# The opening of an attention-and-MLP kernel: three query groups on the incoming keys, one tile's statistics on ScalarE, value projections held back

## The chip, the cores and the metric

The kernel runs on one core of one Trainium2 chip. A core has five engines that run side by side: TensorE (PE, matrix products), VectorE (DVE, elementwise work and reductions), ScalarE (ACT, functions such as the exponential), GpSimd (POOL) and SyncE (SP, which here issues every DMA transfer). The metric is the device time of one execution in microseconds (us); less is better. Times are given for several executions of the same kernel, and one further execution was recorded by the hardware profiler.

## The reference: what is computed

One batch of S = 2048 tokens with D = 1024 features goes through a block of two branches. All inputs are bf16.

```python
xn  = layernorm(x)                        # over the 1024 features, no scale or shift
# branch A: attention with 32 heads of 32
q, k, v = split(xn @ wqkv)                # wqkv is 1024 x 3072
p   = softmax(q @ k.T * 32 ** -0.5)       # per head, 2048 x 2048, not masked
s   = (p @ v, heads side by side) @ wo
# branch B: an MLP on a second normalisation
y   = layernorm(xn)
g   = silu(gelu_tanh(y @ w1 + b1) @ w2 + b2)   # 1024 -> 3584 -> 1024
out = x + s * g
```

The exponentials of the softmax are 32 x 2048 x 2048 elements. They run on ScalarE in 1024 instructions of 128 partitions by 1024 elements.

## The kernel before

The program is not written as loops that run on the chip. A planner in Python (`_Plan`) is given operations with the data that they read and write, an assumed duration and a priority. `run` plays them through with these assumed times and fixes one order for each engine; `settle` derives the semaphore waits, and `emit` writes the instructions. On the chip each engine works through its list strictly in that order: an instruction whose data has not come yet holds up all that stand behind it on its engine.

**Tiles.** Tokens are cut into 16 tiles of 128 (`t`), or 8 pairs of 256 (`n`, `kp` for keys, `qb` for queries). Heads are cut into 8 groups of four (`hg`). A *unit* is one head group, one query pair and one key pair: eight score matmuls (line 809) into two pairs of PSUM banks, then two exponentials (line 818) into a slot of `P`. A *product* (`pvs`, kind "pv") collects over the eight key pairs of one query pair: eight small matmuls a unit with V (`v_fn`) and the sums of the softmax. The sums come either from eight more small matmuls a unit with ones (`plain`, line 893), or from pairwise adds on VectorE (`tree`, lines 835 and 852) and a few matmuls at the end. Only one product is open at a time.

**The opening.** For each tile `load_x` (line 614) brings 128 rows. VectorE takes statistics in two halves (line 759, `bn_stats`) and joins them (line 761); the epsilon is added (line 765), GpSimd raises to the power -1/2 (line 767), and VectorE normalises into a buffer in `gw` (line 736). The tile is then turned so that features lie on partitions (`xnT`): tiles 0 to 3 by TensorE (line 723) with a copy on ScalarE (line 726), the other tiles by a DMA transpose that SP issues (line 740). From `xnT` come, for the first head group, the keys of a token pair (`k_item`, copied out of PSUM by ScalarE on line 712), the queries (`q_item`, copied by VectorE on line 702, or 512 tokens at once with `qk_item`, line 692), and the values of the first two head groups (`v_item`, copied by VectorE on line 680). Projections of 128 rows run through `mm` (line 608). These items, the products and later the MLP's items share PSUM banks 6 and 7; the scores have banks 0 to 5.

In the first head group two query pairs are worked on together while the keys come in. The order of the units is

```python
order0 = [(0, 0), (0, 1), (1, 0), (1, 1)] + [(qb, kp) for kp in range(2, NKP) for qb in range(2)]
```

as (query pair, key pair), so 16 units, and each has its own slot of `P`: ten are the slots of the whole run, three lie in the buffer of `w1` and three in that of `w2`, which are not needed yet. From the 17th unit on, slots 0 to 9 are used in turn. The other six query pairs and the other seven head groups follow one after the other, with their sums in trees on VectorE.

**What sets the order.** For TensorE the planner prefers a score unit that is ready, then a product or an item by position (`pos`) and due time; an item of kind "pro" with `pos` below 0.2 (keys and queries) goes ahead of a product. While TensorE has nothing ready, it is given *fillers*, small matmuls on the identity (line 658). For VectorE, ScalarE and SP it takes the ready operation with the lowest priority number and, among equals, the one that was added first. When it chooses, an operation whose input has only just been produced counts as ready some 115 to 220 ns after the producer's end, and another one may be started in the meantime. The loads of tiles 10 to 15 wait for earlier tiles to be normalised.

The planner also has pseudo-random jitter, by 30 us of planned time and by the index of the operation; it is switched on for the third such stretch only.

## Time and profile before

| | us |
|---|---|
| median of three runs | 1039.95 |
| lowest, highest | 1039.22, 1040.24 |
| the profiled execution's own time | 1039.56 |
| span of the profiled execution | 1037.7 |
| ScalarE busy | 1014.2 |
| TensorE busy | 999.4 |
| VectorE busy | 948.0 |
| mean granted TensorE clock | 0.998 of full speed |

How to read the profile: PE is matmul, PEld the load of matmul weights (it overlaps PE), SPq the issue of DMAs by SyncE. A row of the timeline gives the start in us, the duration of the merged instructions in us, engine, line, operation, written and read tile, and the count `x`; a bracket holds the idle time of that engine just before, and what ended it. Neighbouring instructions overlap a little, so a merged row is shorter than count times the mean of one. A row of busy time by stretch gives the stretch and its length, then the busy time and instructions of PE, PEld, DVE, ACT and POOL, the granted clock, the share of the DMA engines in use and GB/s. A row of a group of instructions gives count, busy us in all, mean ns of one, and the idle time before them with what ended it. A row of DMA issues gives count, size and the median us from issue to landing. The chain that ended last is followed back from the last instruction, at each step to what released it.

### The profile page before, as it was taken

To read this page: it belongs to the slowest core of one execution; us is meant where nothing else is said; L and a number is where in the kernel's file an instruction comes from. 1 tells how busy PE (TensorE), PEld (TensorE's weight loads), DVE (VectorE), ACT (ScalarE), POOL (GpSimd) and SP (SyncE) were. 2 spreads that over 40 slices of the span, in tenths; PEclk is the share of its full clock that TensorE was granted. 3 is DMA by queue.
4 is the path that set the end of the run, shared out by engine and by line. 5 is a ranking of instruction groups with operands and counts; after the bars stand their busy time and mean duration, and the time that the engine had idled before them with its cause. 6 is when DMAs were issued, how large, how long until landed. Compare 5 with 4: busy or idle time off the path is not lost.

```text
span 1037.7 us, 31413 instructions
## 1 busy us (share of the span) xinstructions
PE 999.4 (96%) x14064; PEld 637.6 (61%) x14129; DVE 948.0 (91%) x1314; ACT 1014.2 (98%) x1089; POOL 11.0 (1%) x20
## 2 busy tenths in 40 slices
PE   9999999999999999999999999999999999999996
PEld 7556556666665676666565665666656655654442
DVE  8579999899899999987999999998999799788887
ACT  5899999999999999999999999999999999999996
POOL 1200000000000000000000000000000000000000
PEclk9999999999999999999999999999999999999999
DMA  8985747455656686456375677554456643573321
GB/s 191 206 224 169 190 131 209 122 150 160 180 164 167 174 227 175 129 159 176 106 174 153 179 203 183 164 161 139 135 156 190 197 139 141 165 235 117 111 75 52
DMA packets 318199, 167.99 MB, mean 162 GB/s; under 512 B 56688, under 2 KB 306032, under 8 KB 318064
## 3 DMA queue, kind: packets, MB, share of 16 engines
q1 hardware_dynamic: 318064, 165.98, 58.1%
q8 instruction: 111, 1.82, 0.8%
q14 instruction: 24, 0.20, 0.1%
HBM read 146.55 MB, written 12.06 MB: 153 GB/s over the span
## 4 chain that ended last, share of the span: by engine, by line
ACT 94%; DVE 3%; PE 2%; DMA 1%; issue 0%; POOL 0%; SPq 0%
ACT P L818 86%; ACT ut L1003 5%; ACT gw L1030 1%; DVE stats L759 1%; PE ps L608 1%; DMA hT<-in_A_x_dram 1%; ACT w1r L818 1%; ACT w2r L818 1%; DMA xnT<-gw 0%; DVE gw L736 0%; PE ps L809 0%; PE ps L603 0%; DVE hT L1247 0%; POOL lnp L767 0%; DVE mv L761 0%
## 5 line engine op out<-in xcount | busy, mean ns | idle before, releaser
L818 ACT ACTIVATE P<-ps 128x1024 bf16<-128x1024 f32 x1012 | 944.4, 1249 | 3.7 <-PE ps L809 3.7
L835 DVE TENSOR_TENSOR PA<-P 128x2048 bf16<-128x2048 bf16 x178 | 216.0, 1217 | 32.9 <-ACT P L818 31.9
L608 PE MATMUL ps<-yT,w1r 128*128 128x256 bf16 x1792 | 227.5, 273 | 0.2 <-DVE hT L988 0.2
L608 PE MATMUL ps<-w2r,hT 128*128 128x256 bf16 x1792 | 222.8, 273 | 1.8 <-DVE gw L1023 1.7
L809 PE MATMUL ps<-QKT 32*128 32x256 bf16 x4096 | 203.3, 273 | 16.4 <-ACT P L818 14.1
L852 DVE TENSOR_TENSOR PR<-PR,PA 128x2048 bf16<-128x2048 bf16 x178 | 215.5, 1212 | 1.3
L608 PEld LDWEIGHTS ps<-yT,w1r 128*128 128x128 bf16 x1792 | 163.9, 98 | 52.9 <-issue 28.7
L608 PEld LDWEIGHTS ps<-w2r,hT 128*128 128x128 bf16 x1792 | 163.4, 98 | 50.3 <-issue 30.2
L809 PEld LDWEIGHTS ps<-QKT 32*128 32x128 bf16 x4096 | 60.6, 92 | 148.9 <-ACT P L818 145.2
L603 PE MATMUL ps<-P,V 128*32 128x256 bf16 x4048 | 137.8, 274 | 0.6 <-ACT P L818 0.6
L608 PE MATMUL ps<-xnT,wqk 128*128 128x512 bf16 (+1 forms) x502 | 119.2, 364 | 4.3 <-issue 1.1
L603 PEld LDWEIGHTS ps<-P,V 128*32 128x32 bf16 x4048 | 96.2, 96 | 30.7 <-issue 21.4
L608 PE MATMUL ps<-wv,xnT 128*128 128x256 bf16 (+1 forms) x576 | 86.6, 285 | 2.2 <-DVE V L680 1.2
L608 PEld LDWEIGHTS ps<-xnT,wqk 128*128 128x128 bf16 x552 | 48.0, 98 | 53.0 <-issue 16.9
L988 DVE TENSOR_TENSOR hT<-ps,b1T 128x512 bf16<-128x512 f32 x112 | 76.6, 684 | 1.5 <-PE ps L608 0.8
L835 DVE TENSOR_TENSOR PR<-P 128x2048 bf16<-128x2048 bf16 x62 | 75.4, 1216 | 1.2 <-ACT P L818 0.2
L608 PEld LDWEIGHTS ps<-wv,xnT 128*128 128x128 bf16 x576 | 52.5, 98 | 24.6 <-issue 9.9
L1003 ACT ACTIVATE ut<-ut 128x2048 bf16<-128x2048 bf16 (+1 forms) x32 | 61.2, 1923 | 0.0
L692 DVE CAST QKT<-ps 128x512 bf16<-128x512 f32 x59 | 40.3, 683 | 3.0 <-PE ps L608 2.8
L907 DVE STREAM_TRANSPOSE nt<-ps 128x256 f32<-128x256 f32 x64 | 28.3, 443 | 11.8 <-PE ps L603 11.7
L1000 DVE TENSOR_TENSOR ut<-hT 128x2048 bf16<-128x2048 bf16 (+1 forms) x32 | 34.5, 1082 | 0.2
L1005 DVE TENSOR_TENSOR hT<-ut,hT 128x2048 bf16<-128x2048 bf16 (+1 forms) x32 | 34.5, 1079 | 0.1
(76 smaller groups left out, 535.5 us busy)
## 6 DMA issues: line engine op xcount, KB each, us to landing
w1r<-in_B_w_dram SPq DMA_DIRECT2D x112, 512.0 KB, 4.3
w2r<-in_B_w_dram SPq DMA_DIRECT2D x128, 448.0 KB, 4.3
hT<-in_A_x_dram SPq DMA_DIRECT2D x20, 256.0 KB, 3.7
wqk<-in_A_wqkv_dram SPq DMA_DIRECT2D x16, 256.0 KB, 3.4
yst<-in_A_x_dram SPq DMA_DIRECT2D x16, 256.0 KB, 4.6
g_scratch<-gw SPq DMA_DIRECT2D x32, 128.0 KB, 4.1
o_scratch<-ot SPq DMA_DIRECT2D x56, 64.0 KB, 3.6
xnT<-o_scratch SPq DMA_DIRECT2D x7, 512.0 KB, 5.9
```

What stands on the lines that cost most here:

```text
L603: ins = e.matmul(dst(j), lhsT=lhsT(j), rhs=rhs(j), start=start, stop=stop, tile_position=(0, 32 * j), skip_group_check=True)
L608: return e.matmul(dst, lhsT=lhsT, rhs=rhs, start=start, stop=stop, skip_group_check=True)
L692: dve(lambda e: e.tensor_copy(QKT[sl][:, which, tq * 512:(tq + 1) * 512], bank(it.bank)), c_ps(512), [], [(nm, sl, 2 * tq), (nm, sl, 2 * t ...
L809: ins = e.matmul(bank(b0[j], kk * 256, (kk + 1) * 256), lhsT=QKT[sl][32 * j:32 * j + 32, 1, kb * 128:(kb + 1) * 128], rhs=QKT[sl][32 * j:3 ...
L818: x = act(lambda e, h=h: e.activation(Pt[pi][:, 2 * h:2 * h + 2].rearrange("p j k q -> p (j k q)"), ps[:, pr[h] * 1024:(pr[h] + 1) * 1024] ...
L835: return dve(lambda e: e.tensor_tensor(dst[:].rearrange("p u j q -> p (u j) q"), src[:].rearrange("p u j k q -> p (u j) k q")[:, :, 0, :], ...
L852: return dve(lambda e: e.tensor_tensor(fl3(pr), fl3(pr), fl3(PA[i]), op=ALU.add), c_b16(2048), [("PA", i), tok], [tok], 3.2)
L907: dve(lambda e: e.transpose(nt_t[:], bank(pv.bank, 256, 512)), c_ps(256) + 120, [], [("nt",)], prio, pv)
L988: dve(lambda e: e.tensor_tensor(hT[:, hs], bank(it.bank).rearrange("p (k t) -> p k t", k=2), b1T[:, 2 * pi:2 * pi + 2].unsqueeze(2).to_bro ...
L1000: dve(lambda e: e.tensor_tensor(u_, x_, x_, op=ALU.mult), c_b16(n), hs_, [("ut", ui)], 3)
L1003: act(lambda e: e.activation(u_, u_, ACT.Tanh, scale=GC), c_acts(n), [("ut", ui)], [("ut", ui)], 1)
L1005: dve(lambda e: e.tensor_tensor(x_, u_, x_, op=ALU.mult), c_b16(n), [("ut", ui)] + hs_, hs_, 3)
```

## The change

The change touches the opening, and with it the order that the planner gives to everything behind.

1. *Loads.* Tiles 2 and 3 are loaded ahead of the key and query weights, where they came behind them.
2. *Statistics of tile 1.* They move from VectorE to ScalarE: a Copy and a Square over 1024 elements, each with an accumulated sum, give the mean and the mean square. Three operations of one column on VectorE form the variance. Tiles 2 and 3 now have a power of their own each, and the condition that held back tile 2's statistics until tile 1 is normalised is gone.
3. *ScalarE's copy of tile 1* out of PSUM is cut in two halves, and the data `xnT` is tracked by tile and by block of 128 features, so that projections can start on the first half.
4. *VectorE's order.* Aggregates get a better priority, and in the first 16 us of planned time the planner lets VectorE wait up to 130 ns (220 ns for a normalise) for a nearly ready operation of better priority rather than start a statistic. The assumed duration of a normalise goes from 60 to 118 ns over its base.
5. *Three query groups.* The third query pair joins from the third key pair on. Its first four units get four more slots of `P`, in memory not used yet (one in V, one in the second Q/K buffer, two in `hT` where tiles 6 to 9 were loaded), and its sums are done by `plain` on TensorE. The queries of pairs 2 and 3 become two items of 256 tokens in place of one of 512.
6. *Values.* Value item `n` of the first head groups is not offered until `6 + n` score units have been issued.

```diff
@@ pick
+            if e == "DVE" and best is not None and 1 <= best.prio <= 1.2 and t < 16000.0:
+                for r, _, o in soon[e]:
+                    if r < t + (220.0 if o.prio > 0.96 else 130.0) and o.prio < best.prio - 0.04 and not o.dead:
+                        wake(r, e)
+                        return None
@@ next_dense
-                if h < len(q):
+                if h < len(q) and q[h].hold <= S["s"]:
@@ the kernel
-        NTR, NWARM = 4, 8
+        NTR, NWARM, NG0, AT = 4, 8, 3, 1
...
+        Pt.append(V[:, 2].rearrange("p t n -> p (t n)").rearrange("p (j k q) -> p j k q", j=4, k=2))
+        Pt.append(QKT[1][:, 0].rearrange("p (j k q) -> p j k q", j=4, k=2))
...
+        for i in range(2):
+            Pt.append(h_flat[:, (3 + i) * 2048:(4 + i) * 2048].rearrange("p (j k q) -> p j k q", j=4, k=2))
...
-        load_x(0)
-        load_x(1)
+        for t in range(NTR):
+            load_x(t)
         wk0 = load_qk(0, 1)
         wq0 = load_qk(0, 0)
-        load_x(2)
-        load_x(3)
...
-            act(lambda e: e.activation(xnT[:, :, t * 128:(t + 1) * 128],
-                                       bankb(it.bank).rearrange("p (c t) -> p c t", c=DC), ACT.Copy),
-                c_act(1024), [tk], [("xnT", t)], 0, it)
+            for lo, hi in ((0, 4), (4, 8)) if t == 1 else ((0, 8),):
+                act(lambda e, lo=lo, hi=hi: e.activation(xnT[:, lo:hi, t * 128:(t + 1) * 128],
+                                                         bankb(it.bank)[:, lo * 128:hi * 128].rearrange("p (c t) -> p c t", t=128),
+                                                         ACT.Copy),
+                    c_act((hi - lo) * 128), [tk], [("xnT", t, c) for c in range(lo, hi)], 0, it)
...
-            groups = [(2 * n,), (2 * n + 1,)] if n == 0 else [(2 * n, 2 * n + 1)]
+            groups = [(2 * n,), (2 * n + 1,)] if n < 2 else [(2 * n, 2 * n + 1)]
             for ts in groups:
+                if ts == (AT,):
+                    for k, f, sc in ((0, ACT.Copy, 1.0 / D), (1, ACT.Square, D ** -0.5)):
+                        act(lambda e, k=k, f=f, sc=sc: e.activation(
+                            fl3(PA[0])[:, k * 1024:(k + 1) * 1024], xst[AT], f, scale=sc, accum_out=mv[:, AT, k:k + 1]),
+                            c_acts(1024) + 93, [XS(AT)], [("st", AT, k)], 1)
+                    dve(lambda e: e.tensor_tensor(lnp[:, AT:AT + 1, 2], mv[:, AT:AT + 1, 0], mv[:, AT:AT + 1, 0], op=ALU.mult), 65,
+                        [("st", AT, 0)], [("s2",)], 0.95)
+                    dve(lambda e: e.scalar_tensor_tensor(lnp[:, AT:AT + 1, 0], mv[:, AT:AT + 1, 1], EPS, lnp[:, AT:AT + 1, 2], op0=ALU.add,
+                                                         op1=ALU.subtract), 65,
+                        [("st", AT, 1), ("s2",)], [("ve", AT)], 0.95)
+                    dve(lambda e: e.tensor_tensor(mv[:, AT:AT + 1, 1], mv[:, AT:AT + 1, 1], lnp[:, AT:AT + 1, 2], op=ALU.subtract), 65,
+                        [("st", AT, 1), ("s2",)], [("mv", AT)], 1.1)
...
-                            605, [XS(t)], [("st", t, c)], 1.2, extra=[first[1]] if t == 2 else [])
+                            605, [XS(t)], [("st", t, c)], 1.2)
...
+            if n < NG0:
                 pro_q.append(q_item(n))
...
+                if n == 3:
+                    q0_q.append(q_item(3, "q0", 6.0))
+                else:
+                    q0_q.append(qk_item(0, 0, n // 2, wq0, (0.5, 14.0, 28.0)[n // 2 - 1]))
+                q0_q[-1].due = 16 * (n // 2) + (8 if n == 3 else 0)
...
             plan.dense["v0"].append(v_item(0, n, "pro", 0.2 + 0.01 * n))
+            plan.dense["v0"][-1].hold = 6 + 1 * n
...
-        order0 = [(0, 0), (0, 1), (1, 0), (1, 1)] + [(qb, kp) for kp in range(2, NKP) for qb in range(2)]
+        order0 = [(0, 0), (0, 1), (1, 0), (1, 1), (0, 2), (1, 2), (2, 0), (2, 1)]
+        for kp in range(3, NKP):
+            order0 += [(0, kp), (1, kp)]
+            if kp in (3, 4):
+                order0.append((2, kp - 1))
...
-            got[(qb, kp)] = unit(0, qb, kp, pvs[qb])
+            got[(qb, kp)] = unit(0, qb, kp, pvs[qb], home=16 + kp if qb == 2 else None)
...
-        for qb in range(2):
+        for qb in range(NG0):
+            if qb == 2:
+                for kp in range(4, NKP):
+                    got[(2, kp)] = unit(0, 2, kp, pvs[2])
```

65 lines of the change are left out of this document (38 added, 27 removed).

## The prediction

> **What bounds the kernel now.** I read the page first (busy shares and the chain that ended last), then the busy time by stretch, then ScalarE's own timeline.
>
> ```profile
> PE 999.4 (96%) x14064; PEld 637.6 (61%) x14129; DVE 948.0 (91%) x1314; ACT 1014.2 (98%) x1089; POOL 11.0 (1%) x20
> ACT 94%; DVE 3%; PE 2%; DMA 1%; issue 0%; POOL 0%; SPq 0%
> ```
> ```profile
> 0.00:10.00 10.00, 8.62 (x106) 8.29 (x107) 5.94 (x16) 2.95 (x4) 2.14 (x8) 1.00 0.88 249
> 10.00:20.00 10.00, 9.73 (x133) 7.97 (x130) 10.00 (x27) 5.84 (x8) 1.73 (x3) 1.00 0.64 134
> 20.00:30.00 10.00, 8.82 (x95) 5.87 (x94) 8.66 (x21) 9.23 (x12) 1.07 (x2) 1.00 1.05 242
> 30.00:40.00 10.00, 8.82 (x96) 6.00 (x95) 8.64 (x22) 7.95 (x10) 3.28 (x7) 1.00 1.06 210
> 40.00:50.00 10.00, 10.00 (x171) 6.18 (x174) 2.90 (x6) 9.50 (x13) 2.74 (x2) 1.00 0.91 155
> 80.00:1037.00 957.00, 924.19 (x12995) 585.26 (x13053) 889.30 (x1194) 948.71 (x1013) 0.00 (x0) 1.00 0.56 158
> ```
> The chain is ScalarE's exponentials for 94% of the span. In each row of stretches the fourth busy time is ScalarE's. It has 14.5 us of idle before 50 us (7.05, 4.16, 0.77, 2.05, 0.50). After 80 us it lacks 8.3 us, nearly all of it the end. So an edit of the first 50 us is worth what it takes out of ScalarE's idle time there, provided that the rest stays gapless.
>
> ```profile
> 0.72 1.28 ACT L643 ACT_TABLE_LOAD   x1 [0.72 <-PEq L1306]
> 8.53 1.94 ACT L726 ACTIVATE xnT<-ps 128x1024 bf16<-128x1024 bf16 x2 [6.32 <-PE ps L723]
> 12.48 0.38 ACT L712 ACTIVATE QKT<-ps 128x256 bf16<-128x256 f32 x1 [2.01 <-PE ps L608]
> 13.37 1.94 ACT L818 ACTIVATE P<-ps 128x1024 bf16<-128x1024 f32 x2 [0.50 <-PE ps L809]
> 18.28 0.38 ACT L712 ACTIVATE QKT<-ps 128x256 bf16<-128x256 f32 x1 [1.14 <-PE ps L608]
> 19.17 5.63 ACT L818 ACTIVATE P<-ps 128x1024 bf16<-128x1024 f32 x6 [0.51 <-PE ps L809]
> 24.83 0.39 ACT L712 ACTIVATE QKT<-ps 128x256 bf16<-128x256 f32 x1
> 25.91 3.77 ACT L818 ACTIVATE P<-ps 128x1024 bf16<-128x1024 f32 x4 [0.69 <-PE ps L809]
> 29.54 0.42 ACT L712 ACTIVATE QKT<-ps 128x256 bf16<-128x256 f32 x1
> 31.03 2.85 ACT L818 ACTIVATE P<-ps 128x1024 bf16<-128x1024 f32 x3 [1.07 <-PE ps L809]
> 33.76 0.40 ACT L712 ACTIVATE QKT<-ps 128x256 bf16<-128x256 f32 x1
> 37.81 1.94 ACT L818 ACTIVATE P<-ps 128x1024 bf16<-128x1024 f32 x2 [0.90 <-PE ps L809]
> 39.87 0.38 ACT L712 ACTIVATE QKT<-ps 128x256 bf16<-128x256 f32 x1
> 40.76 2.85 ACT L818 ACTIVATE w1r<-ps 128x1024 bf16<-128x1024 f32 x3 [0.50 <-PE ps L809]
> ```
> Each L712 row is a key pair (256 keys) arriving, each L818 row the exponentials it allows. With two query groups a key pair feeds four exponentials, 3.7 us, and pairs arrive every 4 to 6.5 us. Hence the brackets: after the third pair (25.91) the waits are 1.07, 0.90 and 0.50, 2.47 us in all. The third pair itself is the tightest supply, so I look at what makes it late:
>
> ```profile
> 4.00 1.88 DVE L759 BATCH_NORM_STATS2 stats<-hT 128x6 f32<-128x512 bf16 x3 [2.68 <-DMA hT<-in_A_x_dram]
> 8.40 2.47 DVE L759 BATCH_NORM_STATS2 stats<-hT 128x6 f32<-128x512 bf16 x4
> 15.41 1.28 DVE L759 BATCH_NORM_STATS2 stats<-hT 128x6 f32<-128x512 bf16 x2
> 16.61 0.99 DVE L736 TENSOR_SCALAR gw<-hT,mv,lnp 128x1024 bf16<-128x1024 bf16 x2
> 18.58 2.26 SPq L740 DMA_TRANSPOSE xnT<-gw  x1
> 22.43 1.21 PEld L608 LDWEIGHTS ps<-wv,xnT 128*128 128x128 bf16 x12 [0.21 <-issue]
> 23.65 0.86 PEld L608 LDWEIGHTS ps<-xnT,wqk 128*128 128x128 bf16 x8
> ```
> ```profile
> xnT<-gw SPq DMA_TRANSPOSE x1, 4.0
> ```
> VectorE runs without a pause from 10 to 20 us (10.00 of 10). Tiles 4 and 5 are normalised from 16.61. The second of their transposes is issued at 18.58 and lands 4.0 us later: near 22.6. The keys' matmuls start only at 23.65, because TensorE is inside a value projection. That is 1.05 us of waiting behind values nobody needs yet.
>
> **The change, part by part.**
>
> Loads. Tiles 2 and 3 go ahead of the key and query weights on SP's queue; the number of transfers stays. The query weights then land about two tiles later. From these rows the DMA moves some 340 GB/s, so 0.77 us for a tile of 256 KB:
>
> ```profile
> 6.00:8.00 2.00, 2.00 (x33) 1.83 (x30) 1.60 (x6) 0.00 (x0) 1.18 (x2) 1.00 1.04 338
> wqk<-in_A_wqkv_dram SPq DMA_DIRECT2D x2, 256.0 KB, 4.6
> ```
> The weights were issued by 2.1 us and land near 7; 1.5 us later is 8.5, before tile 1 is transposed (9.1 or later). Cost nothing, and there is a cover of 2 us, below.
>
> Tile 1's statistics on ScalarE. Two passes of 1024 elements are added. The nearest rows are L726 (1.03 us) and the tanh of L1030:
>
> ```profile
> L1030 ACT ACTIVATE gw<-gw 128x1024 f32<-128x1024 bf16 x16 | 20.5, 1279 | 0.0
> L726 ACT ACTIVATE xnT<-ps 128x1024 bf16<-128x1024 bf16 x4 | 3.9, 1028 | 6.3 <-PE ps L723 6.3
> ```
> So 2.1 to 2.6 us; I take 2.1, as the outputs are bf16 like L726's. They lie in the 6.32 us gap ahead of 8.53, at 4.7 to 6.8 (tile 0 lands at 4.00, tile 1 one tile later, by the 0.77 above). VectorE loses two statistics of 0.62 (four in 2.47) and an aggregate, and gains four one-column instructions, which I set against the aggregate: minus 1.2 us. Its normalise then waits for the same power and small step as before, 0.7 us: near 7.5, where it was 7.8. So the first exponential comes at 12.0 to 13.4 instead of 13.37. I count that gain as nothing: with two key pairs' four units (7.4 us), two pairs of L726 (3.9) and two key copies (0.6), 11.9 us in all, from about 7.4 (tile 0 no longer waits behind two of tile 1's statistics: 1.1 us before 8.53) and with 1.9 us of waits, ScalarE is through by 21.2 to 23 and then waits for the third pair. Splitting tile 1's copy in two adds one instruction's overhead, 0.1 us, inside that wait.
>
> VectorE's order. The planner now idles it up to 0.13 or 0.22 us rather than start a 0.62 us statistic ahead of a nearly ready aggregate or normalise. Before, 15 statistics ran before tile 4's normalise at 16.61, five of them not needed for it once tile 1 is gone. Of the other three, 0 to 2 are saved (0 to 1.2 us), and four waits of up to 0.22 are paid (0 to 0.9). With the 1.2 us above, tile 4 is normalised between 0.3 and 2.4 us earlier. I take 1.3, the middle.
>
> Values held back. Item n waits until 6+n score units are issued. The 1.05 us at 23.65 goes, and so do the value matmuls ahead of the scores behind the 1.07 and 0.90 us gaps:
>
> ```profile
> 30.58 0.40 PE L809 MATMUL ps<-QKT 32*128 32x256 bf16 x8
> 36.60 0.83 PE L608 MATMUL ps<-wv,xnT 128*128 128x256 bf16 x6 [1.04 <-DMA xnT<-gw]
> 37.37 0.40 PE L809 MATMUL ps<-QKT 32*128 32x256 bf16 x8
> ```
> At 36.60 a value item was begun whose transposed tile had not landed; the scores at 37.37 stood behind it. So the third pair's exponentials move from 25.91 by 1.3 + 1.05 = 2.35 us to 23.55 (bounds: 1.3 and 3.4 us earlier).
>
> Third query group. From the third pair on the groups are three: four units at that pair, three at each of the next two. That is 7.4 us of exponentials from 23.55, then 5.6 and 5.6, each with 0.3 for a key copy. ScalarE needs the fourth pair at 31, the fifth at 37, the sixth at 43; before they came at 29.54, 33.76 and 39.87, and tiles are not later now. All three later waits lose their cause: 2.47 us. The third group's sums leave VectorE's trees (seven adds of 1.21 us) for TensorE, 64 matmuls at 0.05 us each, 3.2 us:
>
> ```profile
> L603 PE MATMUL ps<-P,ones 128*32 128x256 bf16 x208 | 10.3, 274 | 0.0
> L852 DVE TENSOR_TENSOR PR<-PR,PA 128x2048 bf16<-128x2048 bf16 x178 | 215.5, 1212 | 1.3
> ```
> What hides the 3.2 us is TensorE's 33 us of idle after 80 us (957 less 924.19); if that were gone, they would all be paid.
>
> Sum: 2.35 + 2.47 = 4.8 us. The planner believes transposes land earlier than they do (36.60 shows it), and a key item now stands where the value item did. I leave 0.5 us for such a stall (bounds 0 and 1.5; the nearest row is the 0.90 gap, once in five pairs). Gain 4.3 us, bounds 1.3 + 2.47 - 1.5 = 2.3 and 3.4 + 2.47 = 5.9. The profiled execution took 1039.56 us (span 1037.7 and 1.9 around it), 0.4 below the median 1039.95. It becomes 1035.3, the median 1035.6; this case's own range is 1034.0 to 1037.7.
>
> **Rivals.**
>
> Square is not in the loaded table set. Then two loads of the kind at 0.72 (1.28 us) come on ScalarE. Its work before the third pair ends at 23.8 or later: 0.3 to 2 us lost, about 1036.7. For it: no row uses Square. Against: copies, exponentials and tanh ran with one load. The Trainium skill ("ScalarE: Activation LUTs", section "What ACT_TABLE_LOAD costs") gives 1283 ns for the load, as measured here, and adds a drain: 2.66 us a switch, so by it two cost 5.3 us, ScalarE is through at 26.5, and the time would be 1038.5. The same page lists cheap functions in every set, which speaks against a switch; no run here shows Square.
>
> The third pair is not earlier: idling and extra statistics eat VectorE's saving, and the key items wait for the fifth tile's transpose. Only 2.47 less 0.5 is left: 1038.0.
>
> In-order stalls return: each of the five key pairs from the third stops TensorE for the 1.04 us of 36.60 and ScalarE for 0.7 of it. Then 4.8 - 3.5 = 1.3 us are left, 1038.7. For it: the plan's landing times are too early. Against: among the old trace's rows only 36.60 shows a stall that long.
>
> Slower: the held-back values make the first value product late. Only one such product is open at a time, and the second group's first slot of P is rewritten by the 23rd unit: 18 units of 1.85 and five key copies of 0.28 after 23.55, near 58.2 us. The first product must be done a unit before, so its eighth value item by about 57. Later than that ScalarE waits one for one; the gain is gone at 62, and the kernel is measurably slower past 64. With one item per three units (5.6 us) from 25.4 on, the eighth ends at 66: 9 us of waiting against 4.8 gained, 1044.1. Before, the eighth was this late already:
>
> ```profile
> 53.39 0.69 DVE L680 CAST V<-ps 128x512 bf16<-128x512 f32 x1 [6.96 <-PE ps L608]
> ```
> Against: from 23.6 to 57 TensorE has 33 us, and eight value items (16 matmuls of 0.11, by the 12 in 1.21 at 22.43: 14.1), five key and two query items of 8 (6.2), 17 units' scores (5.6) and the first product (128 small matmuls at 0.03 to 0.05: 3.8 to 6.4) make 30 to 32.
>
> **How the numbers follow.** Forecast 0.62, table switch 0.07, third pair not earlier 0.09, stalls 0.12, late values 0.10. The range 1033.9 to 1039.0 takes in all but the last and some spill. A run of this kernel can tell about 0.2% (2.1 us) from no change: faster means under 1037.9. The forecast gives 0.61 of that, the switch 0.06, the next two 0.06 together: 0.73. Slower is the last case, 0.10, and 0.01 of mishap; 0.16 remain within 0.2%.
>
> **What would show it.** ScalarE's timeline: two new passes between 4.5 and 7, the third key copy near 22.5 with its exponentials near 23.5, and no bracket above 0.5 us after that. ScalarE's idle before 50 us should fall from 14.5 to about 9.6 with 2.1 more of work. TensorE: no value matmuls before 25, the eighth cast by 57. Waits of ScalarE on score matmuls after 25 us, a second table load, or a wait of exponentials on a value product would each make the prediction wrong.

## The result, and the profile after

The changed kernel takes 1037.91 us (median of 16 runs, 1035.57 to 1041.34) against 1040.14 us for the kernel before on the same chips (16 runs, 1039.22 to 1043.1): a ratio of 0.9978, 95% interval 0.997 to 0.9987. It is 2.2 us faster where 4.3 were forecast; 1037.91 lies inside the range and outside the forecast's own (1034.0 to 1037.7). The profiled execution took 1038.8 us with a span of 1037.0, 0.9 above the median, so it is one of the longer executions of this kernel.

The page of the changed kernel, busy shares and the chain that ended last:

```profile
PE 1000.8 (97%) x14096; PEld 638.6 (62%) x14161; DVE 940.6 (91%) x1308; ACT 1017.2 (98%) x1094; POOL 11.5 (1%) x21
ACT 85%; PE 10%; DMA 2%; DVE 2%; issue 1%; SPq 0%; POOL 0%
```

ScalarE has 3.0 us more work than before (1014.2) and in exchange less idle time. The chain now passes through TensorE for 10% of the span (2% before). That is some 100 us, far more than ScalarE is idle, so the chain does not say where ScalarE waits. The stretches do. Their columns are, as before, the stretch, its length, and the busy time (count) of TensorE, weight loads, VectorE, ScalarE and GpSimd, then clock, DMA share and GB/s. First the changed kernel:

```profile
0.00:10.00 10.00, 7.89 (x98) 7.40 (x99) 5.89 (x19) 5.12 (x8) 2.86 (x9) 1.00 0.85 236
10.00:20.00 10.00, 9.37 (x133) 7.70 (x134) 9.60 (x23) 8.04 (x12) 1.26 (x2) 1.00 0.65 187
20.00:30.00 10.00, 7.70 (x94) 5.04 (x92) 7.68 (x21) 8.85 (x13) 2.10 (x3) 1.00 0.70 173
30.00:40.00 10.00, 8.93 (x101) 6.20 (x103) 8.88 (x20) 9.08 (x13) 0.70 (x1) 1.00 1.14 231
40.00:50.00 10.00, 9.76 (x110) 6.82 (x109) 4.21 (x9) 9.89 (x12) 4.62 (x6) 1.00 0.86 105
50.00:60.00 10.00, 9.99 (x267) 6.90 (x269) 2.83 (x7) 9.90 (x12) 0.00 (x0) 1.00 1.10 197
60.00:80.00 20.00, 17.93 (x313) 10.31 (x313) 13.00 (x21) 18.54 (x21) 0.00 (x0) 1.00 0.85 241
```

and the one row of the kernel before that was not shown yet and matters:

```profile
60.00:80.00 20.00, 19.79 (x252) 11.80 (x253) 18.14 (x25) 20.00 (x23) 0.00 (x0) 1.00 0.79 208
```

ScalarE's idle time before 50 us fell from 14.5 to 9.0 us (4.88, 1.96, 1.15, 0.92, 0.11). But between 60 and 80 us, where it had none, it has 1.46 us, and TensorE stood for 2.07 us there (0.21 before). ScalarE's timeline of the changed kernel names each piece. L769 is the new statistics, L722 a key copy, L855 the exponentials; start, busy time, and in brackets the idle time in front and what ended it:

```profile
4.31 1.06 ACT L769 ACTIVATE PA<-hT 128x1024 bf16<-128x1024 bf16 x1 [2.09 <-DMA hT<-in_A_x_dram]
...
5.36 1.04 ACT L769 ACTIVATE PA<-hT 128x1024 bf16<-128x1024 bf16 x1
...
13.26 1.02 ACT L855 ACTIVATE P<-ps 128x1024 bf16<-128x1024 f32 x1 [0.50 <-PE ps L846]
...
15.08 1.03 ACT L855 ACTIVATE P<-ps 128x1024 bf16<-128x1024 f32 x1
...
17.23 4.69 ACT L855 ACTIVATE P<-ps 128x1024 bf16<-128x1024 f32 x5 [0.51 <-PE ps L846]
23.07 0.38 ACT L722 ACTIVATE QKT<-ps 128x256 bf16<-128x256 f32 x1 [1.15 <-PE ps L617]
23.35 4.68 ACT L855 ACTIVATE P<-ps 128x1024 bf16<-128x1024 f32 x5
...
38.67 1.02 ACT L855 ACTIVATE P<-ps 128x1024 bf16<-128x1024 f32 x1 [0.92 <-PE ps L846]
...
64.68 3.77 ACT L855 ACTIVATE P<-ps 128x1024 bf16<-128x1024 f32 x4 [0.56 <-PE ps L846]
69.34 30.53 ACT L855 ACTIVATE P<-ps 128x1024 bf16<-128x1024 f32 x33 [0.89 <-PE ps L846]
```

Read against the rows of before, the account of the gain is this.

| piece | forecast | measured | how the measured number comes out |
|---|---|---|---|
| third key pair | 2.35 | 1.63 | the row of exponentials begins at 23.35, not 25.91: 2.56; but only 7 are done by then (1 + 1 + 5), not 8 (2 + 6), so the first in that row is still the second pair's eighth, worth 0.93 |
| later waits | 2.47 - 0.5 | 1.55 | 1.07 + 0.90 + 0.50 before, 0.92 at 38.67 now |
| after 60 us | 0 | -1.45 | 0.56 and 0.89 are new |
| sum | 4.3 | 1.73 | idle time says about the same: 14.53 before 80 us, now 10.58, less some 2.3 of added work (the statistics take 4.31 to 6.50, the split copy about 0.1): 1.6 to 1.7 |

So ScalarE is 1.7 us ahead at 80 us in this execution. At the end of the exponentials it is 0.85 ahead: they end at 1027.14 before and at 1026.29 in the changed kernel. There is hardly any idle time between (ScalarE is busy for 939.93 of the 940 us from 80 to 1020), so the other 0.85 us went into instructions that took a little longer, some 0.1% on average. The two profiled executions are 0.76 us apart and the medians 2.2; whether this last loss is in the other executions too is not shown.

**Why the eighth exponential is still to be done at 23.35.** TensorE's timeline (L617 is projections, L846 scores), and ScalarE's from the exponential after it on:

```profile
20.29 0.40 PE L846 MATMUL ps<-QKT 32*128 32x256 bf16 x8
21.98 1.70 PE L617 MATMUL ps<-xnT,wqk 128*128 128x256 bf16 x14 [1.30 <-DMA xnT<-gw]
23.62 0.40 PE L846 MATMUL ps<-QKT 32*128 32x256 bf16 x8
```
```profile
24.25 3.78 ACT L855 ACTIVATE P<-ps 128x1024 bf16<-128x1024 f32 x4
```

The scores at 20.29 are the fourth unit's, the last of the first two key pairs, and they end at 20.69. The eighth exponential could have run at 21.92, when ScalarE fell idle. But in ScalarE's list the third pair's key copy stands ahead of it, and that copy waits until 23.07 for key matmuls which TensorE began as soon as their tile had landed (its wait of 1.30 us). So a ready exponential waited in line on ScalarE. The third pair's own scores follow its key copy at 23.62, and its own exponentials begin at 24.25, 1.66 us earlier than before (25.91). The run below with transposes planned to land later has the other order: all eight are done, the key copy comes at 23.14 and the third pair's exponentials at 24.03. By that row the wrong order itself costs this pair only about 0.2 us. The rest of what is missing against the forecast is that the keys come at 23.07 and not near 22.5.

**Where the 0.92 us at 38.67 comes from.** Here it is TensorE's list. First TensorE and SyncE's queue (SPq) of the changed kernel:

```profile
37.91 0.38 PE L617 MATMUL ps<-xnT,wqk 128*128 128x256 bf16 x2 [1.07 <-DMA xnT<-gw]
```
```profile
21.89 5.98 SPq L752 DMA_TRANSPOSE xnT<-gw  x4
27.92 2.00 SPq L626 DMA_DIRECT2D hT<-in_A_x_dram  x4
30.21 4.15 SPq L752 DMA_TRANSPOSE xnT<-gw  x2
```

and SyncE's queue before:

```profile
24.78 1.06 SPq L614 DMA_DIRECT2D hT<-in_A_x_dram  x2
25.88 2.95 SPq L740 DMA_TRANSPOSE xnT<-gw  x2
```

Before, two loads alternate with two transposes, and these are the loads of tiles 12 and 13. Now four transposes go in a row, so those loads start 3.1 us later (27.92 for 24.78), and then four loads of 256 KB go ahead of the transposes of tiles 10 and 11. These two transposes land 6.5 us after their issue (median of the two), where they took 4.2 before. They are issued 1.9 us earlier than before, though (30.21 for 32.13), so the sixth pair is not late: its key copy is at 39.59, and was at 39.87. What counts is that TensorE waits at 37.91 for its tile while the fifth pair's scores, whose keys were copied at 32.65, stand behind. It is the stall of 36.60 in the kernel before, with key matmuls where a value projection stood.

**Where the 1.45 us after 60 us comes from.** ScalarE waits there for score matmuls, and TensorE in front of them for nothing that the profile shows (`issue`). Its weight loads (PEld) inside a run of small value-product matmuls:

```profile
63.46 0.12 PEld L612 LDWEIGHTS ps<-V,ones 128*32 128x32 bf16 x6 [1.27 <-issue]
68.56 0.11 PEld L612 LDWEIGHTS ps<-P,ones 128*32 128x32 bf16 x6 [1.16 <-issue]
```

Each pause cuts a group of eight equal instructions into two and six. The experiments below are mostly about these.

### The profile page after: what moved, and what is told of

The parts are those of the page before. It is cut to its first block, busy times and chain, and to the rows that moved or that the text cites. A ratio compares the mean times of both kernels' runs of the same rounds, so it can differ in the third digit from the quotient of the medians.

```text
span 1037.0 us, 31480 instructions
## 1 busy us (share of the span) xinstructions
PE 1000.8 (97%) x14096; PEld 638.6 (62%) x14161; DVE 940.6 (91%) x1308; ACT 1017.2 (98%) x1094; POOL 11.5 (1%) x21
## 3 DMA queue, kind: packets, MB, share of 16 engines
q8 instruction: 111, 1.82, 0.8%
## 4 chain that ended last, share of the span: by engine, by line
ACT 85%; PE 10%; DMA 2%; DVE 2%; issue 1%; SPq 0%; POOL 0%
ACT P L855 78%; PE ps L617 6%; ACT ut L1037 5%; PE ps L612 3%; PE ps L846 2%; DMA xnT<-gw 1%; ACT gw L1064 1%; DMA w2r<-in_B_w_dram 1%; DVE stats L785 1%; DMA hT<-in_A_x_dram 0%; DVE gw L748 0%; DVE hT L1293 0%; DVE V L690 0%; DVE hT L1287 0%; DVE mv L787 0%
## 5 line engine op out<-in xcount | busy, mean ns | idle before, releaser
L855 ACT ACTIVATE P<-ps 128x1024 bf16<-128x1024 f32 x1004 | 937.4, 1236 | 3.6 <-PE ps L846 3.4
L872 DVE TENSOR_TENSOR PA<-P 128x2048 bf16<-128x2048 bf16 x175 | 212.3, 1216 | 38.3 <-ACT P L855 37.7
L617 PE MATMUL ps<-yT,w1r 128*128 128x256 bf16 x1792 | 228.5, 273 | 1.0 <-DVE hT L1022 0.7
L617 PE MATMUL ps<-w2r,hT 128*128 128x256 bf16 x1792 | 223.2, 273 | 0.5 <-DMA w2r<-in_B_w_dram 0.2
L846 PE MATMUL ps<-QKT 32*128 32x256 bf16 x4096 | 203.3, 273 | 13.8 <-ACT P L855 10.9
L886 DVE TENSOR_TENSOR PR<-PR,PA 128x2048 bf16<-128x2048 bf16 x175 | 211.6, 1210 | 1.2
L617 PEld LDWEIGHTS ps<-yT,w1r 128*128 128x128 bf16 x1792 | 164.1, 98 | 54.5 <-issue 29.3
L617 PEld LDWEIGHTS ps<-w2r,hT 128*128 128x128 bf16 x1792 | 163.4, 98 | 50.0 <-issue 31.3
L846 PEld LDWEIGHTS ps<-QKT 32*128 32x128 bf16 x4096 | 60.7, 92 | 144.3 <-ACT P L855 137.3
L617 PE MATMUL ps<-xnT,wqk 128*128 128x512 bf16 (+1 forms) x511 | 119.1, 360 | 6.5 <-DMA xnT<-gw 2.4
L612 PEld LDWEIGHTS ps<-P,V 128*32 128x32 bf16 x4016 | 95.0, 96 | 31.8 <-issue 22.5
L617 PE MATMUL ps<-wv,xnT 128*128 128x256 bf16 (+1 forms) x576 | 87.1, 285 | 0.5 <-DMA xnT<-gw 0.2
L617 PEld LDWEIGHTS ps<-xnT,wqk 128*128 128x128 bf16 x560 | 49.6, 98 | 53.3 <-issue 14.1
L617 PEld LDWEIGHTS ps<-wv,xnT 128*128 128x128 bf16 x576 | 52.4, 98 | 24.1 <-issue 11.4
```

Source lines behind the costliest of these rows:

```text
L612: ins = e.matmul(dst(j), lhsT=lhsT(j), rhs=rhs(j), start=start, stop=stop, tile_position=(0, 32 * j), skip_group_check=True)
L617: return e.matmul(dst, lhsT=lhsT, rhs=rhs, start=start, stop=stop, skip_group_check=True)
L846: ins = e.matmul(bank(b0[j], kk * 256, (kk + 1) * 256), lhsT=QKT[sl][32 * j:32 * j + 32, 1, kb * 128:(kb + 1) * 128], rhs=QKT[sl][32 * j:3 ...
L855: x = act(lambda e, h=h: e.activation(Pt[pi][:, 2 * h:2 * h + 2].rearrange("p j k q -> p (j k q)"), ps[:, pr[h] * 1024:(pr[h] + 1) * 1024] ...
L872: return dve(lambda e: e.tensor_tensor(dst[:].rearrange("p u j q -> p (u j) q"), src[:].rearrange("p u j k q -> p (u j) k q")[:, :, 0, :], ...
L886: return dve(lambda e: e.tensor_tensor(fl3(pr), fl3(pr), fl3(PA[i]), op=ALU.add), c_b16(2048), [("PA", i), tok], [tok], 3.2)
```

## The experiments

My theory when the runs began: the gain of the opening is real, and three things take part of it back: TensorE's order at 38 us, SyncE's queue behind it, and the pauses after 60 us, which come from the delivery of instructions while the loads of the MLP's weights (w1r, w2r) fill the DMA. "The hold" is the holding back of the value items (part 6 of the change). The rival for the pauses was a hidden dependency of particular instructions; the rival for the whole was that the parts do not need each other.

**The changed kernel again.** No edit.

> The changed kernel once more, as the measure for the others beside it. Theory (fetch): TensorE's two pauses of 1.27 and 1.16 us near 62 and 68 us, inside a run of small matmuls, are waits for the next block of instructions while the weight loads fill the DMA engines; so they stand at the same two places of its instruction list in every execution, 256 instructions apart, and differ in length: 0.5 to 2 us each. Rival (chance disturbance of one execution): no pause over 0.5 us at those places. Both: third key pair's exponentials at 23.35, a wait of ScalarE of about 0.9 us near 38 us, time near 1037.9.

Measured: 1038.33 us (11 runs, 1036.81 to 1039.67), ratio 0.9983 (0.9975 to 0.9992). ScalarE's waits after the third pair:

```profile
58.62 9.30 ACT L855 ACTIVATE P<-ps 128x1024 bf16<-128x1024 f32 x10 [0.47 <-PE ps L846]
69.21 30.53 ACT L855 ACTIVATE P<-ps 128x1024 bf16<-128x1024 f32 x33 [1.29 <-PE ps L846]
```

The wait at 38 us is absent in this execution (the two transposes landed in 5.7 us), so it depends on how a transfer happens to land. The pauses after 859 and 987 weight loads are there again, 0.45 and 1.70 us, with a third of 0.66 us after 731. The two waits shown are 1.76 us.

**Transposes planned to land later.** If the stalls in TensorE's order are what is missing, a plan with more honest landing times should win.

```diff
-                    [("xnb", t % 4)], [("xnT", t, c) for c in range(DC)], prio=0, rate=300.0, occ=1300, lat=1000)
+                    [("xnb", t % 4)], [("xnT", t, c) for c in range(DC)], prio=0, rate=300.0, occ=1300, lat=2500)
```

> The planner is told that a DMA transpose of a tile lands 1.5 us later (2.5 in place of 1.0 us after the transfer), nothing else. Theory (order): ScalarE's 0.92 us wait at 38.67 comes from scores standing behind two key matmuls whose tile has not landed; with the scores ahead the wait is under 0.3 us and the time about 0.9 us below the changed kernel, near 1037.0. Rival (supply): the fifth and sixth key pairs themselves are late, ScalarE waits as long on the key copy or on the next scores, time near 1037.9.

Measured: 1041.58 us (11 runs, 1039.27 to 1042.91), ratio 1.0012 (1.0002 to 1.0021). Slower, where a gain was expected. The wait near 38 us did shrink to 0.35, but these rows are new:

```profile
61.59 5.61 ACT L855 ACTIVATE P<-ps 128x1024 bf16<-128x1024 f32 x6 [1.93 <-PE ps L612]
68.25 3.77 ACT L855 ACTIVATE P<-ps 128x1024 bf16<-128x1024 f32 x4 [1.05 <-PE ps L846]
```

The first is the prediction's slower rival: with key matmuls planned later, value items slip too, the eighth value cast (VectorE's copy of values out of PSUM) comes at 58.32 (49.86 in the changed kernel), and ScalarE waits 1.93 us for the first value product to free its slot of P. The second stands behind a pause of TensorE (1.20 us), and a longer one follows (2.53 us, ScalarE waits 2.26).

**Weights fetched later.** The first w1r and w2r loads wait until the third group's product has been copied out, so that the DMA is quiet while the three products run. Nothing of the opening changes.

```diff
         def copy_values(pv, g):
-            dve(lambda e: e.tensor_copy(nv_t[g % 2][:], ...
+            return dve(lambda e: e.tensor_copy(nv_t[g % 2][:], ...
...
-            dma(f"w1{gi}", ..., lat=3100.0)
+            dma(f"w1{gi}", ..., lat=3100.0, extra=late3 if p < NW1R else ())
...
+            ex = late3 if nw2["n"] <= NW2R else ()
-            dma(f"w2{i}", ..., lat=3100.0)
+            dma(f"w2{i}", ..., lat=3100.0, extra=ex)
...
-            copy_values(pvs[qb], qb)
+            late3 = [copy_values(pvs[qb], qb)]
```

> The first three loads of w1 and the first four of w2 are held until the third group's product is copied out (near 69 us), so that hardly any transfer runs while the three products are formed. Theory (fetch): TensorE's two pauses near 62 and 68 us fall under 0.3 us, ScalarE's waits of 0.56 and 0.89 us near 64 and 69 go, about 1.4 us below the changed kernel, near 1036.5. Rival (the third product's own operands or its PSUM bank cause the pauses): the pauses stay. Second rival: the MLP that starts some 7 us later costs more than is won, time 1038 or above.

Measured: 1035.74 us (5 runs, 1035.45 to 1037.54), ratio 0.9962 (0.9949 to 0.9974), and 2.6 us below the changed kernel run beside it (1.4 below was expected). ScalarE from 57 to 98 us:

```profile
56.78 41.62 ACT L855 ACTIVATE P<-ps 128x1024 bf16<-128x1024 f32 x45
```

Forty-five exponentials without a wait: no such pause is left on TensorE. What changed there is the DMA. The stretch of the middle pause, the changed kernel and then this one (last two columns: DMA share and GB/s):

```profile
62.00:64.00 2.00, 1.01 (x34) 0.72 (x32) 1.62 (x5) 2.00 (x3) 0.00 (x0) 1.00 0.99 323
```
```profile
62.00:64.00 2.00, 1.78 (x56) 1.05 (x56) 1.83 (x6) 2.00 (x3) 0.00 (x0) 1.00 0.18 61
```

The removed waits are 1.76 us of the 2.6, by one execution of each; the profiled one here is the longest of the five (1037.54) and has a wait of 0.57 at 39.30. The rest is not accounted for by a wait.

**The same edit on the kernel before.** Late weights might be good by themselves. The diff is the same five edits on the old file, with two products instead of three.

> Control: the kernel before with its first loads of w1 and w2 held until its second product is copied out. Theory (fetch): before, TensorE takes 6 to 8 us for a block of 256 instructions there and never pauses over 0.4 us, so there is nothing to win: within 1 us of before, or above it where the MLP starts late. Rival (less traffic helps the opening whatever the instructions do): 2 us or more below before.

Measured: 1040.12 us (11 runs, 1039.37 to 1040.83), ratio 1.0 (0.9992 to 1.0009). No difference, as expected: the kernel before has no pause of this kind above 0.44 us, and so none to lose.

**Traffic put back.** Late weights as above, and eight loads of 256 KB that nothing reads fill the DMA in the same stretch. If the pauses come from the transfers and not from what they carry, they return.

```diff
+            if qb == 0:
+                for i in range(8):
+                    dst = fl_ut[i % 4]
+                    dma(f"dm{i % 4}", lambda e, ...: e.dma_start(dst, x2[i * 128:(i + 1) * 128, :]), 262144, [],
+                        [("dm", i % 4)], prio=1, rate=390.0, extra=late3)
```

> Late first weights, and eight transfers of 256 KB of x into a buffer not yet in use, issued when the first product is copied out (near 56 us); nothing reads what they bring. Theory (fetch): any transfer delays the blocks of instructions: a pause of 0.4 to 2 us comes back after TensorE's 859th weight load, perhaps after the 731st or 987th, and with it 0.5 to 1.5 us of ScalarE's waiting, time 1036.3 to 1037.5. Rival (the weights themselves, their buffers or their semaphores made the pauses): no pause over 0.4 us, time as with late weights, 1035.7.

Measured: 1035.97 us (5 runs, 1035.61 to 1036.28), ratio 0.9959 (0.9946 to 0.9971).

```profile
55.96 0.11 PEld L612 LDWEIGHTS ps<-P,ones 128*32 128x32 bf16 x6 [0.59 <-issue]
61.88 0.11 PEld L612 LDWEIGHTS ps<-V,ones 128*32 128x32 bf16 x6 [0.99 <-issue]
```

The pauses came back, with no other cause added than traffic. ScalarE waited 0.40 and 0.29 us behind them, but the time is that of late weights alone, where 1036.3 to 1037.5 was expected. Traffic is shown as what brings the pauses. What these two cost is not: 0.69 us is less than the interval of this run (1.3 us to each side).

**The opening with two groups.** The other parts without the third group, first without the hold and then with it.

```diff
-        NTR, NWARM, NG0, AT = 4, 8, 3, 1
+        NTR, NWARM, NG0, AT = 4, 8, 2, 1
-            plan.dense["v0"][-1].hold = 6 + 1 * n
-        order0 = [(0, 0), (0, 1), (1, 0), (1, 1), (0, 2), (1, 2), (2, 0), (2, 1)]
-        ...
+        order0 = [(0, 0), (0, 1), (1, 0), (1, 1)] + [(qb, kp) for kp in range(2, NKP) for qb in range(2)]
```

(and the fourth query item as it was before; the second run keeps the line with the hold.)

> The opening alone: load order, tile 1's statistics on ScalarE, VectorE's order; two query groups as before, values not held back. Theory: keys of the third pair come as early as in the changed kernel, their exponentials near 23.5 to 24.5 us (25.91 before), but with two groups the waits for the later pairs stay (2.5 us before) or grow by what was won: 0 to 1.5 us below the kernel before. TensorE's list has no third product, so no pause over 0.45 us at the 256-instruction marks. Rival (the opening carries the whole gain): 2 us or more below before.

> The changed kernel without the third query group. Theory: no pauses over 0.45 us of TensorE at the block marks, as the small matmuls of a third product are gone; but the key pairs after the third come at 4 to 6 us and feed 3.7 us of exponentials, so ScalarE waits 3 to 5 us in all between 24 and 50 us; time within 1 us of before. Rival (the third group is not needed once values are held): ScalarE waits under 2 us there, time as the changed kernel or below it, 1037 to 1038.

Measured: 1047.04 us (5 runs, 1045.2 to 1048.56), ratio 1.0068 (1.0056 to 1.008), and with the hold 1042.91 us (5 runs, 1042.05 to 1045.25), ratio 1.0034 (1.0022 to 1.0047). The longest wait of ScalarE without the hold, then with it:

```profile
51.31 0.38 ACT L722 ACTIVATE QKT<-ps 128x256 bf16<-128x256 f32 x1 [3.58 <-PE ps L617]
```
```profile
46.91 0.38 ACT L722 ACTIVATE QKT<-ps 128x256 bf16<-128x256 f32 x1 [3.60 <-PE ps L617]
```

The waits were expected in kind but not in size: the times are 7.4 and 3.2 us above the kernel before run beside them, where at most 0 and 1 were expected. The opening makes the seventh and eighth key pairs later, in both (the eighth's copy is at 55.87 and 51.47, and was at 47.37), and with two groups ScalarE has nothing to do meanwhile. Neither has a pause of the kind seen after 60 us.

**Three groups with the old opening.** The load order, the second tile's statistics on VectorE, VectorE's waiting rule and its priorities are those of before; three groups and the hold stay.

```diff
-        NTR, NWARM, NG0, AT = 4, 8, 3, 1
+        NTR, NWARM, NG0, AT = 4, 8, 3, -1
-        for t in range(NTR):
-            load_x(t)
+        load_x(0)
+        load_x(1)
         wk0 = load_qk(0, 1)
         wq0 = load_qk(0, 0)
+        load_x(2)
+        load_x(3)
...
```

> Three query groups and values held back, on the opening as it was before. Theory: third pair's exponentials at 24.9 (25.91 less the 1.05 us of value matmuls); later waits under 1 us in all; pauses of TensorE at its 859th and 987th weight load (give or take the fillers) cost 1 to 2 us again; time 0.5 to 1.5 us below before, near 1039. Rival (the groups carry the whole gain): 2 us or more below before.

Measured: 1043.34 us (12 runs, 1039.23 to 1046.16), ratio 1.0029 (1.0018 to 1.0039).

```profile
73.52 0.10 PEld L607 LDWEIGHTS ps<-P,V 128*32 128x32 bf16 x2 [3.24 <-issue]
```

That is 3.7 us above the kernel before run beside it, where 0.5 to 1.5 us below was expected. The row is the longest pause of all runs, 3.24 us, in the longest of the twelve executions; ScalarE's wait behind it is 3.64. It also waits 1.27 us at 29 us, behind a tile that has not landed, and 1.18 at 32.

**Value projections not held back.**

```diff
-            plan.dense["v0"][-1].hold = 6 + 1 * n
```

> The changed kernel without the holding back of the value items. Theory (values in the way): value matmuls stand ahead of the third pair's keys again, its exponentials come 0.5 to 1.1 us later than 23.35, and ScalarE waits on scores between 28 and 38 us once or twice more; time about 1 us above the changed kernel, 1038.9. Rival (keys go first anyway, and the third group covers the rest): within 0.3 us of the changed kernel.

Measured: 1044.91 us (5 runs, 1042.72 to 1045.83), ratio 1.0042 (1.003 to 1.0055). The sign was as expected, the size was not: the loss is 6.6 us against the changed kernel run beside it. And it does not lie where I had put the hold's worth. The third pair is not later; ScalarE:

```profile
23.46 3.77 ACT L854 ACTIVATE P<-ps 128x1024 bf16<-128x1024 f32 x4 [0.51 <-PE ps L845]
39.96 0.38 ACT L722 ACTIVATE QKT<-ps 128x256 bf16<-128x256 f32 x1 [2.98 <-PE ps L617]
```

All eight exponentials of the first two pairs are done by 23.46, as the key copy does not stand ahead of the last one in this plan. The waits come later: 2.98 us at 40, while TensorE waits 2.82 us for a tile, and 2.87 at 77 behind a pause of TensorE (2.53 us).

**Late weights, and the last loads of x moved behind the transposes.** Two tries for a version that loses neither to the order at 38 us nor to the pauses. The second also holds values one unit less.

```diff
-                        load_x(t, [first[2 * n - 5]])
+                        load_x(t, [first[2 * n - 5 if n < 7 else 11]])
```

```diff
-            plan.dense["v0"][-1].hold = 6 + 1 * n
+            plan.dense["v0"][-1].hold = 5 + 1 * n
```

> Late first weights, and the loads of tiles 14 and 15 wait for tile 11's normalise in place of tile 9's. Theory (transfers in front): tiles 10 and 11 land 7.5 us after their transposes are issued because four tile loads of 256 KB stand ahead of them; with two of them behind they land about 1.5 us earlier, and ScalarE's wait near 38 us (0.92 in the changed kernel, 0.57 with late weights) goes: 0.5 us below late weights alone, near 1035.2. Rival (tiles 14 and 15 become late instead): a wait on the eighth key pair after 45 us of a like size, time as with late weights or above.

> Late first weights, tiles 14 and 15 loaded behind tile 11, and value item n from the (5+n)th score unit on in place of 6+n. Theory (product late): with the eighth value item before the first product, ScalarE's 0.64 us wait near 59 us goes, no other wait over 0.3 us comes after the third pair, 0.5 us below late weights: near 1035.2. Rival (values in the way): a wait on scores between 25 and 45 us takes its place, 1035.7 or above.

Measured: 1035.69 us (5 runs, 1035.65 to 1036.71), ratio 0.9964 (0.9952 to 0.9976): no difference from late weights alone, where 0.5 us less was expected. The two transposes land in 4.9 us with two loads ahead of them (6.5 with four in the changed kernel, where the expectation has 7.5), and the wait at 38 us is gone; but it is gone in two of the runs without this edit too. The eighth value cast is at 55.73, and a wait of 0.64 us for a slot of P appears at 59.01. With the smaller hold 1037.68 us (10 runs, 1036.97 to 1039.36), ratio 0.9975 (0.9966 to 0.9984): the slot wait is gone, but the time is 2 us longer, where 0.5 us less was expected. A pause is back although the weights are late, and ScalarE waits 1.12 us behind it. The DMA was busy with other transfers just before it (248 GB/s from 56 to 57 us):

```profile
58.17 0.11 PEld L612 LDWEIGHTS ps<-P,V 128*32 128x32 bf16 x5 [1.47 <-issue]
```

**Late weights with the later planned landing.** Separates the two losses of the planned landing: the pauses should go and the slot wait stay.

```diff
-                    ..., prio=0, rate=300.0, occ=1300, lat=1000)
+                    ..., prio=0, rate=300.0, occ=1300, lat=2500)
```

> Late first weights and the later assumed landing of the transposes together. Theory: of the 3.7 us that the later landing lost against the changed kernel, the pauses at the block marks go (two waits of ScalarE of 1.05 and 2.26 us), and the wait of 1.93 us for the first product, whose eighth value item ends at 58 us, stays: 1037.5 to 1038.5. Rival (all of it was the pauses): 1035.7 or below.

Measured: 1038.24 us (11 runs, 1036.18 to 1039.82), ratio 0.9981 (0.9973 to 0.999), within the 1037.5 to 1038.5 expected. No pause of that kind, and one wait after the third pair:

```profile
62.17 28.81 ACT L855 ACTIVATE P<-ps 128x1024 bf16<-128x1024 f32 x31 [2.92 <-PE ps L612]
```

It is the wait for the first product, at 2.92 us and not the 1.93 expected, with the eighth cast at 57.81.

**The granted clock in the runs that lost.** Something besides the order differs in them. The granted clock of TensorE was 0.5 for 3.4 us or twice that, beginning within 2 us of the end of a stop of TensorE of 1.6 to 3 us: in the opening with two groups (6.8 us, with the hold 3.4), in three groups with the old opening (twice 3.4), without the hold (twice 3.4) and in late weights with the later landing (3.4, at 59.5). Opening with two groups, then no hold:

```profile
37.70:44.50 6.80, 6.23 (x40) 3.42 (x41) 1.63 (x5) 3.49 (x5) 0.24 (x1) 0.50 0.75 184
```
```profile
38.30:41.70 3.40, 3.40 (x23) 2.03 (x21) 0.30 (x1) 1.30 (x2) 0.00 (x0) 0.50 0.53 160
```

The kernel before, the changed kernel, its repetition and the run with transposes planned later have no such stretch before the end, though TensorE stands still for 2.25 us once in the last of these. At half clock 6.8 us hold at most 3.4 us less of TensorE's work (an estimate from these rows), so a part of what these runs lose may be this and not the waits themselves. No run separates the two or shows what sets it off.

**What the runs say together.** Against the kernel before: the opening alone costs 0.7%, the opening with the hold 0.3%, three groups with the hold 0.3%, the opening with three groups 0.4%; all together gain 0.2%, and with the weights fetched later 0.4%. With any one of the three left out, the kernel is slower than before; of the single parts only the opening was run alone. The reading that fits the waits: the opening brings the third pair forward and the seventh and eighth back, the third group gives ScalarE work while it waits for these, and the hold decides how late values may be. How much of each loss is the clock is open.

## Why the prediction was right and wrong

**Right: the bound and the place.** ScalarE's idle time in the first 50 us is what changed, and the sign follows from it.

**Right: statistics on ScalarE.** "Two passes of 1024 elements" at 2.1 us: they run from 4.31 to 6.40 (5.36 + 1.04), 2.1 us. A readout of the sum behind each, 0.19 us long and mostly overlapped, makes it 2.2. The first exponential, counted as nothing within 12.0 to 13.4, came at 13.26.

**Right: no table switch.** The only table load of the changed kernel is the one at the start:

```profile
0.72 1.28 ACT L653 ACT_TABLE_LOAD   x1 [0.72 <-PEq L1352]
```

Square with an accumulated sum ran in the table set that was loaded. The Trainium skill ("ScalarE: Activation LUTs", section "Table sets: the hidden batching unit") has cheap functions in every set. It names relu, copy, identity and abs; that Square ran without a load too is what this trace adds.

**Right in direction, too large: the third pair.** Its exponentials were to move by 2.35 us, from 25.91 to 23.55. They moved by 1.66, to 24.25; the row at 23.35 begins with an exponential of the second pair. The key copy moved by 1.76, from 24.83 to 23.07. Of that, tile 4's normalise gave 0.97 us, where I took 1.3:

```profile
15.64 1.00 DVE L748 TENSOR_SCALAR gw<-hT,mv,lnp 128x1024 bf16<-128x1024 bf16 x2 [0.23 <-POOL lnp L794]
```

and the other 0.8 is what came of the 1.05 us that the value matmuls had cost: with them gone, TensorE waits for the tile itself. The rest was lost on ScalarE, where the key copy stands ahead of a ready exponential. The sum had no term for ScalarE's own order.

**Too large by 0.4: "All three later waits lose their cause: 2.47 us", with 0.5 left for stalls.** The cause that was given did go: with three groups the fourth, fifth and sixth pair came in time (29.68, 32.65 and 39.59 for the 31, 37 and 43 needed). What came back is the stall that the prediction itself had named, a key item where the value item stood; it cost 0.92 us, within its bounds of 0 and 1.5, and was absent when the same kernel ran again. So the rival of in-order stalls was right as a mechanism, at two pairs and not at five, once in ScalarE's list and once in TensorE's.

The premise "tiles are not later now" held for these three pairs and failed for the last two. The eighth key pair, after and before:

```profile
51.45 0.38 ACT L722 ACTIVATE QKT<-ps 128x256 bf16<-128x256 f32 x1
```
```profile
47.37 0.47 ACT L712 ACTIVATE QKT<-ps 128x256 bf16<-128x256 f32 x1
```

It came 4.1 us later, and at 51.47 in the run with the opening, the hold and two groups, so it is not the third group that delays it. Three groups cover that delay; the runs with two show it as waits of 3.6 us. I had counted the transfers that pass SyncE without following their order.

**Wrong: "What hides the 3.2 us is TensorE's 33 us of idle after 80 us".** The 64 matmuls of the third group's sums are hidden as work, and TensorE does stand idle enough. What the sentence did not see is that three products now lie back to back from 51 to 69 us, in instructions so short that their delivery stops TensorE when the DMA is full: 1.45 us of waiting, the largest single miss. The prediction had no term for it. That late weights take the pauses and 2.6 us away, and nothing from the kernel before, shows that they matter; that traffic alone brings pauses back shows where they come from. The exact price is not shown, as the traffic run's pauses did not lengthen its time measurably. "No bracket above 0.5 after that" failed at 38.67, 64.68 and 69.34 us.

**The slower rival.** The eighth value cast was at 49.86 in the changed kernel, well before the 57 us that I needed, so it did not happen. It was no empty case: two edits that move value items by 6 to 8 us ran into it, at 0.64 us with the cast at 55.73 and at 1.93 us with the cast at 58.32. If ScalarE waits one for one, the edge is at 55.1 to 56.4, one to two us ahead of the 57 worked out. (One figure of that working is off: a value matmul is 0.10 us by the row it names, not 0.11, so eight items take 12.9 us and not 14.1. The conclusion is the same.)

**An inconsistency.** The sum needs ScalarE's idle time before 50 us to fall by the gain and the added work, 4.3 + 2.1, to 8.1 us. The "about 9.6" given as a sign to look for did not follow from the sum, and that 9.0 was measured is no support for it.

**Luck.** That the time fell inside the range owes something to chance: the range had been widened for other rivals, and the largest loss, the pauses, was in none of them.

## What to carry to other kernels

When inputs are brought forward in a plan with fixed orders, look at the list of each engine that waits for them: does an instruction that is ready stand behind one that is not? Here a ready exponential stood behind a key copy, and ready scores behind key matmuls. A time at which something starts is a gain only together with what is already done by then, so count both. And where an edit puts many very short instructions back to back, look at the rate at which they are used up and at what the DMA does in that stretch, since here the pauses came and went with that traffic.

## What the runs showed of the hardware

**Pauses of TensorE 128 weight loads apart.** In each kernel that has such pauses, they fall after 731, 859 or 987 weight loads (732 by the records of one run), whatever instruction stands there. Weight loads up to just before a pause: the changed kernel, then three groups with the old opening (stretch, length, busy time (count), clock, DMA share, GB/s):

```profile
0.00:63.41 63.41, 41.59 (x859) 1.00 0.90 196
0.00:68.51 68.51, 44.62 (x987) 1.00 0.90 200
```
```profile
0.00:73.47 73.47, 45.76 (x987) 0.98 0.86 201
```

and the times at which the kernel before passes the same counts, without a pause:

```profile
0.00:63.50 63.50, 42.41 (x859) 1.00 0.92 210
0.00:71.80 71.80, 47.09 (x988) 1.00 0.93 216
```

128 weight loads and their 128 matmuls are 256 instructions. The page lists an instruction queue among the DMA queues:

```profile
q8 instruction: 111, 1.82, 0.8%
```

1.82 MB in 111 pieces are 16.4 KB each, 64 bytes for each of 256 instructions. The changed kernel's page counts 14096 matmuls and 14161 weight loads, which make 110.4 blocks of 256, so 111 pieces fit TensorE's instructions alone. So the pauses are read as waiting for the next block; where blocks begin was not seen directly. Pace and traffic go with it: the kernel before takes 8.3 us for the block between these counts and does not pause; the changed kernel takes 5.1 and pauses 1.27 us at its start and 1.16 at its end, with the DMA at 323 GB/s around the first (62 to 64 us); with late weights the blocks up to the same two counts take 4.8 and 4.3 us at 177 and 19 GB/s, without a pause. The pauses seen range from 0.45 to 3.24 us. The Trainium skill ("Runtime: NRT & Kernel Launch", section "Instruction fetch mechanics") tells of blocks of 256 instructions, fetched by the sequencer over a DMA queue of its own. The trace agrees on the 256. It also calls the cost of a block's edge "mostly hidden"; at the edges with a pause here it was not.

**What stays open.** How far ahead a block is asked for was not measured, nor what the pauses of the run with traffic, 0.59 and 0.99 us, cost. One pause came back with the weights late and the hold smaller (1.47 us); other transfers ran then, so late weights alone do not keep the DMA quiet. The changed kernel's runs spread over 5.8 us, those of the kernel before over 3.9; that pauses of changing length do it is argued, not shown.
